# Five K loads and two dk stores of an attention backward kernel, each cut by rows into three transfers

## The chip, the cores and the metric

The kernel runs on one core of a Trainium2 chip. The core has five instruction streams, TensorE (PE, whose weight loads are listed as PEld), VectorE (DVE), ScalarE (ACT), GpSimd (POOL) and SyncE (SP), and 16 DMA engines that move data between HBM and the on-chip SBUF. SP and GpSimd only start transfers here; the DMA engines carry them out. The metric is the device time of one execution in microseconds (us). Before the change the median of three runs is 1271.71 us (1270.49 to 1273.73).

## The reference

The reference is one decode step of softmax attention together with its backward pass. There are 2 x 32 = 64 heads; each has one query row, 8192 keys and values of width 128, all in bfloat16:

```python
B, H, Sq, Sk, D = 2, 32, 1, 8192, 128
def _fwd_reference(q, k, v):
    scale = q.shape[-1] ** -0.5
    scores = jnp.einsum("bhqd,bhkd->bhqk", q, k) * scale
    p = _softmax(scores, axis=-1)
    return jnp.einsum("bhqk,bhkd->bhqd", p, v)

def reference(q, k, v, grad_out):
    _out, _vjp = jax.vjp(_fwd_reference, q, k, v)
    return (_out, *_vjp(grad_out))
```

The outputs are the attention output, dq, dk and dv. K, V, dk and dv are 134 MB each, so 268 MB are read and 268 MB are written; q, grad_out, out and dq are 16 KB each.

## The kernel before, in words

**Tiles.** A head's K (or V) is one tile of 128 rows (the 128 partitions of the SBUF) by 64 x 128 elements: row p holds 64 consecutive keys, 16 KB. A tile is 2 MB. There are twelve such tiles in SBUF (`NTILE = 12`), enough for six heads. Head i+6 is loaded into the tiles of head i, with K and V exchanged (`slot_of`): K of head i+6 goes where V of head i was.

**Work on a head.** TensorE transposes the tile in chunks of 16 keys per row (L220), ScalarE copies each chunk out (L222), and TensorE multiplies it with q or grad_out into scores (L241). VectorE and ScalarE do the softmax. TensorE accumulates out and dq from the original tiles (L401). Then VectorE overwrites the V tile with dv and the K tile with dk (`outer`, L456), and the tile is stored.

**Order.** One loop over chunk steps g interleaves up to four heads, eight steps to a head; every instruction is pinned to its written order on its engine.

**Transfers and their queues.** SP starts all large loads (`load`, L100), in order. Each takes a whole tile, except for K of head 0, which is cut along the row into three. GpSimd starts the stores (L474), in order: dv of head i, dk of head i, dv of head i+1 and so on. Only the last head's stores are cut into quarters and started by SP. A load must wait until the store that frees its tile has landed. Each queue also has eight completion semaphores that it uses in turn, so that a transfer waits for the one eight places before it on its own queue.

**Stores by rows.** `SPREAD` names heads 6, 18, 30, 42 and 54. Their dk is stored by `by_rows` (L89) as two transfers, of 126 and of 2 rows. In this helper `max_dma_last_dim` leaves a row as two pieces of 4096 elements, 8 KB each. Near the start, GpSimd resets the cursor of its transfers and loads 6 of the 64 rows of q (`FIRST = 6`, L112); SP loads the other 58 rows.

Of the kernel before, what the change touches and what calls it, by code (L numbers as in the profile page):

```python
# [20 lines left out]
NTILE = 12  # L21
FIRST = 6
SPREAD = range(6, 60, 12)


@with_exitstack
def kernel(
# [24 lines left out]
    load_eng = nc.sync  # L52
    store_eng = nc.gpsimd
# [26 lines left out]
    def slot_of(i, w):  # L80

        n = 2 * i + w
        return n if n < NTILE else slot_of(i - NTILE // 2, 1 - w)

    def by_rows(eng, dst, src, rows):

        p = 0
        for m in rows:
            pin(eng.dma_start(out=dst[p : p + m], in_=src[p : p + m], max_dma_last_dim=NT * D))  # L89
            p += m  # L90

    def load(i, w, pieces=(NCH,)):
        h = heads[i]
        t = kvp.tile([P, NT, D], BF16, tag=f"kv{slot_of(i, w)}", name="kvt")
        h.tile[w] = t
        src = (v_v if w else k_v)[i]
        c = 0
        for m in pieces:
            n0, n1 = c * CH, (c + m) * CH
            pin(load_eng.dma_start(out=t[:, n0:n1, :], in_=src[:, n0:n1, :]))  # L100
            c += m

    load(0, 0, (1, 1, 2))

    qd_nat = evp.tile([P, CH, P], BF16, tag="ev", name="qd_nat")
    for w, a in enumerate((q, grad_out)):
# [9 lines left out]
        pin(load_eng.dma_start(out=qd_nat[r0:BH, w, :], in_=rows[r0:BH]))  # L116

    load(0, 1)
    for j in range(1, min(NTILE // 2, BH)):
        load(j, 0)  # L120
        load(j, 1)
# [328 lines left out]
    def outer(i, w, c, ends):  # L450

        h = heads[i]
        n0 = c * CH
        shape = [P, CH, D // 2, 2]
        pin(
            nc.vector.tensor_tensor(  # L456
                out=h.tile[w][:, n0 : n0 + CH, :].rearrange("p n (e t) -> p n e t", t=2),
                in0=h.qb[w][:]
                .rearrange("p (e t) -> p e t", t=2)
                .unsqueeze(1)  # L460
                .to_broadcast(shape),
                in1=h.pair[w][:, n0 : n0 + CH, :].unsqueeze(2).to_broadcast(shape),
                op=ALU.mult,
            )
        )
        if c + 1 in ends:
            at = ends.index(c + 1)
            b0, b1 = (ends[at - 1] if at else 0) * CH, (c + 1) * CH
            dst = (dv_v if w else dk_v)[i]
            if w == 0 and i in SPREAD:  # L470
                by_rows(store_eng, dst, h.tile[w], (P - 2, 2))
            else:
                eng = load_eng if len(ends) > 1 else store_eng
                pin(eng.dma_start(out=dst[:, b0:b1, :], in_=h.tile[w][:, b0:b1, :]))  # L474
# [12 lines left out]
    for g in range(SL * BH + O0 + NCH + 4 - SL):  # L487
# [15 lines left out]
        if x := within(O1):  # L503
            outer(x[0], 1, x[1], last if x[0] == BH - 1 else whole)
        if x := within(O0):
            outer(x[0], 0, x[1], last if x[0] == BH - 1 else whole)
        ev = None
        if g < SL * BH:
            i, r = divmod(g, SL)
# [84 lines left out]
```

## Time and profile before

| What | Value |
|---|---|
| median of the runs | 1271.71 us |
| time of the profiled execution | 1271.48 us |
| its span, first to last instruction | 1269.7 us |
| PE / DVE / ACT / POOL busy | 85% / 80% / 43% / 6% |
| HBM read and written over the span | 423 GB/s |
| SP's queue (q1): packets, MB, share of 16 engines | 20172, 272.70, 50.4% |
| GpSimd's queue (q0): packets, MB, share of 16 engines | 19216, 264.25, 49.0% |
| whole-tile store, issue to landing (median) | 66.1 us |
| whole-tile load, issue to landing (median) | 20.1 us (V), 20.3 us (K) |

The span is measured from the first to the last instruction; 1.8 us of the profiled execution lie outside it. A DMA queue's share says how much of the time of all 16 engines its packets took. A packet is one contiguous piece, here mostly a 16 KB row. A busy share of an engine is an average; an idle engine costs nothing unless it is the one that the end waits for.

### The profile page before, as it was taken

The page shows a single profiled execution, that of the slowest core. Times are in us where ns is not written, and L with a number is a line of the kernel's source. Part 1 is how long each engine was busy: PE and PEld are TensorE (multiplying, and loading weights), DVE is VectorE, ACT ScalarE, POOL GpSimd, SP SyncE. Part 2 cuts the span into 40 slices and gives each one's busy share as a digit, 9 for nine tenths or more (in the row PEclk, how much of TensorE's full clock was granted, in tenths as well). Part 3 has the DMA queues.
Part 4 walks back from the last instruction along what each step waited for, and adds up shares of the span by engine and source line. Part 5 has one row for each costly group of instructions (what it writes and reads, how often), then busy time and mean ns, then how long its engine had stood idle before and what let it go on. Part 6 is the DMA issues. An engine that isn't in the chain of part 4 may idle for free.

```text
span 1269.7 us, 24553 instructions
## 1 busy us (share of the span) xinstructions
PE 1073.2 (85%) x10056; PEld 757.9 (60%) x10056; DVE 1020.8 (80%) x2269; ACT 552.0 (43%) x769; POOL 72.9 (6%) x138
## 2 busy tenths in 40 slices
PE   6999999999888997988897888888888889898870
PEld 4666666666656665666565656555655656565540
DVE  3889998998878898788787878788878887796882
ACT  3545444444434444444343444444434444444430
POOL 0000000000000000000000000000000000000000
PEclk9999999999999999899899999999989999998995
DMA  9999999999999999999999999999999999999997
GB/s 392 427 429 428 428 428 429 429 429 429 430 428 429 428 429 432 428 429 429 430 424 425 429 429 428 429 429 428 424 428 431 428 429 429 428 430 426 430 426 294
DMA packets 39501, 538.53 MB, mean 424 GB/s; under 512 B 4956, under 2 KB 4956, under 8 KB 6236
## 3 DMA queue, kind: packets, MB, share of 16 engines
q1 hardware_dynamic: 20172, 272.70, 50.4%
q0 software_dynamic: 19216, 264.25, 49.0%
q8 instruction: 79, 1.29, 0.4%
q14 instruction: 34, 0.28, 0.1%
HBM read 268.47 MB, written 268.47 MB: 423 GB/s over the span
## 4 chain that ended last, share of the span: by engine, by line
DMA 33%; another core or an unknown queue 22%; DVE 17%; PE 13%; issue 9%; ACT 2%; SPq 1%; POOL 1%; ACTq 0%; POOLq 0%; DVEq 0%
DMA kvt<-in_v_dram 18%; DMA kvt<-in_k_dram 10%; DVE kvt L456 9%; PE tp L220 8%; DMA out_dram<-kvt 4%; DVE sel L424 3%; DVE rows L254 2%; PE acc L401 2%; PE raw L241 2%; ACT ev L222 1%; SPq L100 1%; DVE sel L418 1%; PE sw L261 1%; DVE pair L335 1%
## 5 line engine op out<-in xcount | busy, mean ns | idle before, releaser
L222 ACT COPY ev<-tp 128x1024 f32<-128x1024 f32 x512 | 518.6, 1013 | 665.5 <-PE tp L220 659.3
L220 PE MATMUL tp<-ident_f,kvt 128*128 128x128 f32 x4096 | 566.2, 283 | 96.0 <-DMA kvt<-in_v_dram 70.5
L456 DVE TENSOR_TENSOR kvt<-qb,pair 128x2048 bf16<-128x2048 bf16 x512 | 616.9, 1216 | 0.1
L220 PEld LDWEIGHTS tp<-ident_f,kvt 128*128 128x128 f32 x4096 | 470.2, 147 | 216.5 <-issue 170.6
L241 PE MATMUL raw<-ev,qwin 128*32 128x512 bf16 x2048 | 210.3, 400 | 0.0
L254 DVE COPY rows<-raw 128x512 f32<-128x512 f32 x128 | 88.0, 688 | 91.9 <-PE raw L241 91.7
L424 DVE SCALAR_TENSOR_TENSOR sel<-acc,diag,sel 128x128 f32<-128x128 f32 x384 | 134.7, 351 | 13.6
L261 PEld LDWEIGHTS sw<-sel,rows 128*128 128x128 f32 x1024 | 125.5, 193 | 30.4 <-DVE sel L418 15.2
L261 PE MATMUL sw<-sel,rows 128*128 128x16 f32 x1024 | 138.0, 267 | 0.5 <-DVE st L355 0.5
L474 POOL DMA_DIRECT2D out_dram<-kvt x121 | 64.7, 534 | 1106.3 <-DVE kvt L456 507.3
L401 PE MATMUL acc<-kvt,dS_pad 128*32 128x512 bf16 x1024 | 107.3, 410 | 0.8 <-DVE dS_pad L387 0.8
L401 PE MATMUL acc<-kvt,E_pad 128*32 128x512 bf16 x1024 | 103.0, 392 | 0.7 <-DVE E_pad L312 0.7
L202 PE MATMUL sw<-ident_f,qT 128*128 128x128 bf16 x128 | 29.1, 227 | 55.3 <-DVE st L275 55.1
L347 PEld LDWEIGHTS sw<-st,ones 128*128 128x128 f32 x256 | 38.4, 189 | 56.2 <-issue 54.5
L241 PEld LDWEIGHTS <-qwin 128*32 128x32 bf16 x2048 | 54.0, 95 | 5.4 <-issue 1.0
L347 PE MATMUL sw<-st,ones 128*128 128x1 f32 x256 | 49.3, 262 | 0.5 <-DVE st L318 0.5
L280 DVE TENSOR_REDUCE st<-sw 1x1 f32<-1x128 f32 x64 | 17.9, 279 | 37.8 <-PE sw L279 37.8
L401 PEld LDWEIGHTS <-dS_pad 128*32 128x32 bf16 x1024 | 26.4, 94 | 36.2 <-issue 29.1
L401 PEld LDWEIGHTS <-E_pad 128*32 128x32 bf16 x1024 | 26.3, 93 | 33.7 <-issue 28.8
L438 PEld LDWEIGHTS acc<-ones,sel 128*128 128x128 f32 x256 | 39.8, 197 | 8.1 <-DVE sel L424 8.1
L312 DVE CAST E_pad<-E_f 128x64 bf16<-128x64 f32 x64 | 12.5, 195 | 38.9 <-ACT E_f L303 38.9
L418 DVE TENSOR_SCALAR sel<-acc,diag 128x128 f32<-128x128 f32 x128 | 43.7, 342 | 0.0
(53 smaller groups left out, 399.3 us busy)
## 6 DMA issues: line engine op xcount, KB each, us to landing
out_dram<-kvt POOLq DMA_DIRECT2D x121, 2048.0 KB, 66.1
kvt<-in_v_dram SPq DMA_DIRECT2D x64, 2048.0 KB, 20.1
kvt<-in_k_dram SPq DMA_DIRECT2D x63, 2048.0 KB, 20.3
out_dram<-kvt POOLq DMA_DIRECT2D x5, 2016.0 KB, 71.2
out_dram<-kvt SPq DMA_DIRECT2D x8, 512.0 KB, 23.9
kvt<-in_k_dram SPq DMA_DIRECT2D x2, 512.0 KB, 4.3
kvt<-in_k_dram SPq DMA_DIRECT2D x1, 1024.0 KB, 6.9
out_dram<-kvt POOLq DMA_DIRECT2D x5, 32.0 KB, 70.5
```

The source lines that it names most:

```text
L220: pin(nc.tensor.transpose(tp[:, m, :], two, ident_f[:]))
L222: pin(nc.scalar.copy(out=ev[:], in_=tp[:]))
L241: nc.tensor.matmul(h.raw[g * SW : (g + 1) * SW, :], lhsT=qwin[:, w, e, q0 : q0 + SW], rhs=cols[:, b, :, e], start=(c == 0), stop=(c == NCH ...
L254: pin(nc.vector.tensor_copy(out=h.rows[:], in_=h.raw[:]))
L261: nc.tensor.matmul(h.score[w].rearrange("p (n m t) -> p n m t", m=QT, t=2)[:, :, m, :], lhsT=h.rows[:, m * P : (m + 1) * P], rhs=sel4[:].r ...
L347: nc.tensor.matmul(out, lhsT=ones[:].to_broadcast([P, P]), rhs=col, start=True, stop=True)
L401: nc.tensor.matmul(h.acc[w][g : g + CW, :], lhsT=wts[:, n0 : n0 + CW], rhs=rows[:, n0 : n0 + QT, :].rearrange("p n d -> p (n d)"), start=( ...
L418: nc.vector.tensor_scalar(out=h.sel[:], in0=block, scalar1=diag[:, 0:1], scalar2=None, op0=ALU.mult)
L424: nc.vector.scalar_tensor_tensor(out=h.sel[:], in0=block, scalar=diag[:, b : b + 1], in1=h.sel[:], op0=ALU.mult, op1=ALU.add,)
L438: nc.tensor.matmul(h.acc[w][:, 0:1], lhsT=h.sel[:], rhs=ones[:], start=True, stop=True)
L456: nc.vector.tensor_tensor(out=h.tile[w][:, n0 : n0 + CH, :].rearrange("p n (e t) -> p n e t", t=2), in0=h.qb[w][:] .rearrange("p (e t) -> ...
L474: pin(eng.dma_start(out=dst[:, b0:b1, :], in_=h.tile[w][:, b0:b1, :]))
```

## The change

Seven of the whole-tile transfers are cut by rows into three. On SP: K of heads 9, 11, 13, 15 and 17, as 112 rows and two smaller parts. On GpSimd: dk of heads 8 and 12. They all go through `by_rows`, so a row becomes two 8 KB pieces (a part of one row stays in one piece). Order, engines and the work on the data stay as they were. SP starts ten more transfers and GpSimd four more. The lines below the new constants move down by two, those behind the new lines in `load` by five, and those behind the new branch in `outer` by seven.

```diff
 SPREAD = range(6, 60, 12)
+LOAD_ROWS = {9: (112, 8, 8), 11: (112, 12, 4), 13: (112, 14, 2), 15: (112, 10, 6), 17: (112, 15, 1)}
+STORE_ROWS = {8: (112, 8, 8), 12: (112, 12, 4)}
@@ in load
         src = (v_v if w else k_v)[i]
+        if w == 0 and i in LOAD_ROWS:
+            by_rows(load_eng, t, src, LOAD_ROWS[i])
+            return
         c = 0
@@ in outer
             if w == 0 and i in SPREAD:
                 by_rows(store_eng, dst, h.tile[w], (P - 2, 2))
+            elif w == 0 and i in STORE_ROWS:
+                by_rows(store_eng, dst, h.tile[w], STORE_ROWS[i])
             else:
```

## The prediction

> **What bounds the kernel now.** I read the page's slices first, then the DMA table, then the waits of the two issuing queues, then the end in windows.
>
> ```profile
> span 1269.7 us, 24553 instructions
> DMA  9999999999999999999999999999999999999997
> q1 hardware_dynamic: 20172, 272.70, 50.4%
> q0 software_dynamic: 19216, 264.25, 49.0%
> ```
>
> The 16 DMA engines are busy in every slice but the last; the two queues fill 99.4% of their time. No compute engine does (PE 85%, DVE 80%). So bytes per DMA engine set the time. A 16 KB row costs one engine 16384 x 16 x 0.504 x 1269.7 / 272.70 MB = 0.615 us (the packet records: mostly 0.611).
>
> ```profile
> SPq L100 <- DMA out_dram<-kvt: 1126.0, 116, 27.4
> POOL out_dram L474 <- DMA out_dram<-kvt: 104.1, 12, 13.9
> POOL out_dram L89 <- DMA out_dram<-kvt: 1.2, 1, 1.2
> 150.00:250.00 100.00, 93.07 (x896) 65.94 (x889) 90.46 (x202) 49.27 (x68) 7.26 (x13) 0.98 1.01 429
> 250.00:350.00 100.00, 89.43 (x866) 63.53 (x866) 86.48 (x194) 47.45 (x67) 5.85 (x11) 1.00 1.01 429
> ```
>
> SP waits for stores to free tiles nearly all the time; GpSimd lost 104 us to the landing of earlier stores and the DMA share (last column but one) stayed at 1.01 in these windows, in which the stores and most of the loads of the change fall. Waits of the issuers are covered by queued transfers.
>
> ```profile
> 1240.00:1245.00 5.00, 1.00 (x9) 0.13 (x1) 4.89 (x9) 0.00 (x0) 0.00 (x0) 0.50 1.02 433
> 1245.00:1250.00 5.00, 0.90 (x3) 0.63 (x3) 0.72 (x4) 0.00 (x0) 0.00 (x0) 0.50 0.96 401
> 1250.00:1255.00 5.00, 0.00 (x0) 0.00 (x0) 0.00 (x0) 0.00 (x0) 0.00 (x0) 0.50 0.90 374
> 1255.00:1260.00 5.00, 0.00 (x0) 0.00 (x0) 0.00 (x0) 0.00 (x0) 0.00 (x0) 0.50 0.64 267
> 1260.00:1265.00 5.00, 0.00 (x0) 0.00 (x0) 0.00 (x0) 0.00 (x0) 0.00 (x0) 0.50 0.47 193
> 1265.00:1269.70 4.70, 0.00 (x0) 0.00 (x0) 0.00 (x0) 0.00 (x0) 0.00 (x0) 0.50 0.11 42
> ```
>
> Compute is over at 1247 us. From there the DMA share falls in steps: engines run dry one after another, and the last one sets the end. The trace keeps the times of the 16 increments (one per engine) of each transfer. Those of the last small store come at 1251.7, 1253.0, 1254.7, 1254.8, 1255.5, 1257.1, 1259.6, 1259.9, then 1264.3, 1265.8, 1266.3, 1266.4, 1266.5, 1266.7, 1266.8 and 1268.2 us. Eight engines are early, eight late; the mean is 1261.1. A perfectly even spread would save 7.1 us. **So the question is which engines gain rows and which lose them.**
>
> **Which engine gets which row.** I put the packet records into 16 sequences (each packet starts 3 to 4 ns before the end of the one before it on its engine; where two fit, the pattern of eight rows and a 4-byte completion decides). They show: a 128-row transfer is 8 rows per engine; the 58-row load of q on SP went to two engines, 29 rows each; GpSimd's 6-row load put one row on each of six engines, those two among them; each 126-row store put 9 rows on 14 engines, and its 2-row companion one row on each of the other two, the same two all five times. So rows are dealt in equal shares to the largest number of engines, up to 16, that divides them, and GpSimd's small parts go on from where the last ended (14 + 2 = 16 comes back). Of the two spared engines one is slow: its rows took 0.620 us as loads and 0.631 as stores, against 0.612 and 0.615.
>
> **The five loads.** 112 rows are 7 per engine, and a part of m rows one row on each of m engines, instead of 8 on all. If all SP parts start at the same engine, the sums over the five loads, in the order of engines, are +5, +4, +3, +3, +2, +2, +1, +1, -1, -1, -2, -2, -3, -3, -4, -5 rows (21 moved). If they rotate as GpSimd's do, each load deals 16 rows in turn and the sum is 0. The sequences show only one SP transfer that did not use all engines, so both stay possible; I take the same start: it gives the wider bounds, and the kernel resets a cursor for GpSimd alone. Bounds: the last engine gets +5 rows, +3.1 us; at best the eight late ones are the eight that lose, paired as well as can be, and the end moves to 1265.3, -2.9 us. Between them: the two engines of the q load (+5, +4) ended by 1260, so they stay harmless. Of the two that end last, one is among the six of the 6-row load (the sequences leave open which), so with a common start it would get +2 or +3 rows: 1266.8 + 1.2 = 1268.0 up to 1268.2 + 1.8 = 1270.0, against 1268.2 now. That is 0 to +1.8; I take the middle, **+0.9 us**.
>
> [...]
>
> **The two stores.** 7 rows on all engines, then 8 + 8 or 12 + 4 = 16 rows dealt in turn: 0, and the cursor returns. If GpSimd's parts started at one engine instead, this would add at most 2 rows, 1.2 us, either way.
>
> **Packets and completions.** An engine handles some 40 rows of the split loads and 16 of the split stores as two packets: 2 x 0.309 - 0.611 us less one more overlap of 3.5 ns is 3.5 ns each, 0.2 us. 14 more transfers bring 4-byte completions of 9 ns, and the SPREAD windows show some four extra per engine for small parts: under 0.2 us. **+0.4 us** together.
>
> **Issue and waits, costed at nothing.** SP starts ten more transfers at 0.33 us, GpSimd four more at 0.5 to 0.8. The second and third part each wait for the semaphore used eight transfers before; behind them stand the next V load on SP and the next dv store on GpSimd, and K loads of later heads wait for that store. A load there lands 30 us after issue; even with every second K load cut, eight places are some 50 us, so those have landed 20 us earlier. On GpSimd at 190 to 300 us a store lands 43 to 50 us after issue and one is issued every 9.5 us: five in flight, seven with two small ones, under eight. The cover is the queue: from a store's issue to its first increment 20 us pass at 110 us, where the first split load is issued, and 35 from 190 us on. A K load in 8 KB pieces that takes turns with 16 KB store packets takes 16 x (0.306 + 0.608) = 14.6 us instead of 9.7 in the engine; five times 4.9 us later would be 24 us if nothing covered it, but the engine moves stores meanwhile, so what is late next is a dk store by 5 us, inside the 20.
>
> **Sum.** 1271.48 (the profiled execution; the median is 0.23 above) + 0.9 + 0.4 = **1272.8 us**.
>
> **Rival A, slower: the spared pair moves.** If the parts of a split store don't bring GpSimd's cursor back to where it was, the four SPREAD stores after head 12 spare another pair. The slow engine then takes 9 rows instead of 1 four times: 32 x 0.62 = 20 us, and ends at 1259.6 + 20 = 1279.4 instead of 1259.6; with the last engine at 1268.2 that is +11.2, **1283 us**. It decides from two lost SPREADs on (8.6 us of slack are 14 rows). For it: no record shows a part of 8, 12 or 4 on GpSimd. Against: 6, 126 and 2 rows follow the simple count five times.
>
> **Rival B, faster: the late eight are the eight that lose,** and GpSimd's parts start at one engine too: the eight then lose 2, 2, 3, 3, 5, 5, 6 and 7 rows, and paired as well as can be the end moves to 1264.6: -3.6, with the overhead **1268.3 us**. Against: one of the two last engines is near the start. More than 7.1 us less the overhead, 1264.8, no dealing of rows can give.
>
> **Rival C, slower: the cover fails.** A split load or store makes the DMA share drop between 110 and 400 us. It decides once a wait outlasts the 20 to 35 us; GpSimd's longest was 13.9, and one more of that size on top would cost up to its own length: 1277 to **1286 us**. Against: 12 such waits cost no share before.
>
> **How the numbers follow.** Forecast 0.69, A 0.11, B 0.08, C 0.07, something unnamed 0.05. 0.3%, 3.8 us, is about what a measurement of this kernel can tell from no change: 1267.9 to 1275.5. The row bounds of -2.9 and +3.1 with the overhead are 1269.0 to 1275.0, inside it. B lies just inside it as well, and the scatter of the runs (1.6 us) would show it as faster about every second time. So slower 0.20 (A, C and half the unnamed), faster 0.07 (half of B and of the unnamed), same 0.73. The range takes in those bounds, B and the mild end of C, and leaves out A: 1268.0 to 1277.0.
>
> **What would show it.** Right: DMA share 1.01 up to 1240, five K loads of 1792 KB and 14 small parts in the DMA table, increments of the last store that shift by at most 3.1 us each, the two q engines later by 2.5 to 3 us. Wrong: one increment alone 10 us behind all others (A), a window of 100 us below 428 GB/s between 110 and 400 us (C), or all late increments earlier by 2 us or more (B).

## The result, and the profile after

The change made the kernel slower by four to five microseconds. The median of six runs is 1276.36 us (1274.66 to 1278.14) against 1271.47 us (1270.26 to 1273.73) of six runs of the kernel before. The ratio is 1.0039, with a 95% interval of 1.0025 to 1.0053: +4.9 us, between +3.2 and +6.7. The prediction's 1272.8 us was 3.6 us too low. Its range (1268.0 to 1277.0) held the time, but the ratio lies above the 0.3% that it called "no change", though the interval reaches down to 0.25%; to the slower side it had given a chance of 0.20. The profiled execution took 1275.63 us, 4.15 more than that of before; its span grew by 4.2 us.

The page of the kernel after, its first line, its slices of DMA share and of GB/s, and its queues:

```profile
span 1273.9 us, 24586 instructions
DMA  9999999999999999999999999999999999999997
GB/s 392 424 429 429 426 419 411 422 420 420 427 429 428 430 429 428 431 428 428 430 429 427 431 429 428 430 429 427 423 430 428 429 429 430 428 429 427 430 424 295
q1 hardware_dynamic: 20891, 272.70, 50.4%
q0 software_dynamic: 19600, 264.25, 49.0%
```

The bytes of both queues are those of before, the DMA engines are busy throughout as before, and the queues' shares are the same. What moved is the third line: slices 6 to 10 (some 160 to 320 us) carry 411 to 422 GB/s, where before and in most later slices it is 427 to 431. In that stretch the packets of the five loads and the two stores move. The same windows as in the prediction (columns: window, its length, busy time and count on PE, PEld, DVE, ACT and POOL, PE clock, DMA share, GB/s):

```profile
150.00:250.00 100.00, 91.67 (x824) 65.04 (x822) 82.96 (x186) 45.14 (x63) 8.12 (x14) 0.91 1.01 417
250.00:350.00 100.00, 81.96 (x765) 58.06 (x762) 76.73 (x168) 41.46 (x58) 6.23 (x12) 0.93 1.01 422
```

Before, both windows showed a DMA share of 1.01 and 429 GB/s. Now the share is still 1.01 and the GB/s have fallen to 417 and 422. If the engines waited, both would fall. Here only the bytes fell, so the engines were busy and **their packets took longer**. The granted PE clock is lower as well (0.91 and 0.93 against 0.98 and 1.00), and PE did fewer matmuls; but PE was not the bound in either kernel, since the DMA engines had no gap. (A kernel further below, 25 loads in 8 KB pieces, has a clock of 0.86 in a window and keeps 429 GB/s there.)

The packet records say how much longer. Before, a 16 KB packet of a whole tile mostly took 0.611 us and an 8 KB piece 0.309 us. I add up what each packet took above that, and divide by 16 engines; this is called the **excess** from here on.

```
                       excess per engine, us     16 KB and 8 KB packets
                       110-340 us   whole run    over by 60 ns, 110-340 us
before                    0.89         6.23                23
after                     4.66         9.73               341
```

The excess grew by 3.5 us in the whole run, and all of that lies in the stretch of the change. The long packets sit where rows of a split load and rows of a whole load are under way together: 325 of the 341, though only 46% of the packets of the stretch run at such a moment. While a split load is under way and no whole one (11% of the packets), hardly any is long (3 of the 341). Of the 341, 216 belong to stores.

The end of the kernel after:

```profile
1245.00:1250.00 5.00, 1.06 (x9) 0.13 (x1) 4.89 (x9) 0.00 (x0) 0.00 (x0) 0.50 1.01 428
1250.00:1255.00 5.00, 0.90 (x3) 0.63 (x3) 0.78 (x4) 0.00 (x0) 0.00 (x0) 0.50 0.96 402
1255.00:1260.00 5.00, 0.00 (x0) 0.00 (x0) 0.00 (x0) 0.00 (x0) 0.00 (x0) 0.50 0.83 346
1260.00:1265.00 5.00, 0.00 (x0) 0.00 (x0) 0.00 (x0) 0.00 (x0) 0.00 (x0) 0.50 0.60 250
1265.00:1270.00 5.00, 0.00 (x0) 0.00 (x0) 0.00 (x0) 0.00 (x0) 0.00 (x0) 0.50 0.43 176
1270.00:1273.90 3.90, 0.00 (x0) 0.00 (x0) 0.00 (x0) 0.00 (x0) 0.00 (x0) 0.50 0.07 29
```

The shares tell when the average engine ends. After: 1250 + 5 x (0.96 + 0.83 + 0.60 + 0.43) + 3.9 x 0.07 = 1264.4 us. Before, in the same way from the rows in the prediction: 1245 + 5 x (0.96 + 0.90 + 0.64 + 0.47) + 4.7 x 0.11 = 1260.4 us. So **the average engine ends 4.0 us later**, though it moves the same bytes: 3.5 us of excess and about the 0.4 us that the prediction had for packets and completions. (The packets' times alone, added up, grew from 1261.9 to 1266.1 us per engine, 4.2; with some 1,100 more packets, that each overlap the one before by 3.5 ns, 0.2 of this is counted twice.) The last engine's final completion moved from 1267.7 to 1272.4 us, by 4.7. Redealing rows cannot move the average; this alone tells that the main cost is not which engine has which row.

Rows of the DMA waits of the issuing engines in the kernel after (engine, line, what it waited for: us in total, times, longest):

```profile
POOL out_dram L481 <- DMA out_dram<-kvt: 28.6, 3, 11.9
...
SPq L91 <- DMA out_dram<-kvt: 39.4, 5, 9.3
SPq L91 <- DMA kvt<-in_k_dram: 32.8, 4, 10.9
```

The split transfers do wait on SP, up to 10.9 us at a time for an earlier load, by the program for the semaphore that it still holds. With the share at 1.01, none of it reached the DMA engines.

### The profile page after: what moved, and what is told of

Read it like the earlier page. It is cut to its first block, busy times and chain, and to the rows that moved or that the text cites. A ratio compares the mean times of both kernels' runs of the same rounds, so it can differ in the third digit from the quotient of the medians.

```text
span 1273.9 us, 24586 instructions
## 1 busy us (share of the span) xinstructions
PE 1072.7 (84%) x10056; PEld 757.6 (59%) x10056; DVE 1021.0 (80%) x2269; ACT 552.3 (43%) x769; POOL 75.9 (6%) x142
## 4 chain that ended last, share of the span: by engine, by line
DMA 38%; DVE 23%; PE 15%; issue 11%; another core or an unknown queue 10%; ACT 2%; POOL 1%; SPq 0%; ACTq 0%; POOLq 0%; DVEq 0%
DMA kvt<-in_k_dram 24%; DVE kvt L461 12%; DMA kvt<-in_v_dram 10%; PE tp L225 8%; DMA out_dram<-kvt 3%; DVE sel L429 3%; DVE rows L259 2%; PE acc L406 2%; PE raw L246 2%; ACT ev L227 2%; DVE sel L423 1%; PE sw L266 1%; DVE pair L340 1%; DVE dSu L383 1%
```

## The experiments

The first question was which part of the change costs the time; the second, what about a split makes packets longer; the third, which engine ends last. Kernels measured together share runs of the kernel before, so the comparison value differs a little from group to group.

**The five loads alone.**

```diff
-STORE_ROWS = {8: (112, 8, 8), 12: (112, 12, 4)}
+STORE_ROWS = {}
```

> Only the five split loads, stores as before. The changed kernel took 4.9 us longer; in its trace, packets between 110 and 340 us were longer by 3.8 us per DMA engine in all. Theory P (placement: in a 112-row load a row goes through another DMA engine than in a 128-row load, and packets of two engines slow each other): +4 to +5. Theory R (only the dealing of rows counts, the two split stores are the rest): +1.5 to +2.

Measured: 1276.69 us against 1272.43, ratio 1.0033 (1.0020 to 1.0045), +4.3 us. The excess at 110 to 340 us is 5.55 us. This is what theory P expected, and R did not: the loads carry nearly all of the change's cost. The excess is above the 4.66 of the whole change, so from one profiled run to another it can differ by about 1 us.

**The two stores alone.**

```diff
-LOAD_ROWS = {9: (112, 8, 8), 11: (112, 12, 4), 13: (112, 14, 2), 15: (112, 10, 6), 17: (112, 15, 1)}
+LOAD_ROWS = {}
```

> Only the two split stores, loads as before. P and R with loads as the cause: 0 to +0.7. If the stores carry the loss (cursor, completions, packets): +3 to +5.

Measured: 1273.73 us, ratio 1.0009 (1.0000 to 1.0018): +1.3 us by the medians, anything from 0 to 2.3. The expected 0 to +0.7 lies in that interval, the +3 to +5 does not. The excess at 110 to 340 us is 1.45, 0.56 above that of before. Together with the loads (4.3 + 1.3 = 5.6) this agrees with the change's +4.9 within the intervals.

**Five loads cut evenly.** 112 and 16 rows. Going by the counts that the prediction read from the records (128 rows as 8 to an engine, 126 as 9 on 14 engines), I took both parts to be dealt in equal shares to 16 engines, 7 and 1 rows each, so that no engine gains a row.

```diff
-LOAD_ROWS = {9: (112, 8, 8), 11: (112, 12, 4), 13: (112, 14, 2), 15: (112, 10, 6), 17: (112, 15, 1)}
-STORE_ROWS = {8: (112, 8, 8), 12: (112, 12, 4)}
+LOAD_ROWS = {i: (112, 16) for i in range(9, 18, 2)}
+STORE_ROWS = {}
```

> The same five loads cut as 112 and 16 rows, so that every DMA engine gets 8 rows again (7 + 1); stores as before. P, or theory K (8 KB pieces beside 16 KB packets are what slows): +3 to +4.5, packets between 110 and 340 us longer by some 3.8 us per engine. R, or theory N (parts on fewer than 16 engines push the engines out of step): 0 to +0.5.

Measured: 1274.14 us, ratio 1.0014 (1.0005 to 1.0023), +1.7 us. The last engine ends at 1270.4, 2.7 us later than before, with no row gained by that count. That lies between what P or K (+3 to +4.5) and what R or N (0 to +0.5) expected, and decides for neither; but this split costs something, though by that count every engine keeps its eight rows. Between this and the five loads alone are 2.55 us; but the excess differs as well (3.09 against 5.55 us), so that difference cannot be put down to the dealing of rows alone. The stretch of 110 to 340 us in the kernel before and in this one:

```profile
110.00:340.00 230.00, 211.28 (x2041) 149.97 (x2041) 204.64 (x456) 111.87 (x156) 14.71 (x27) 0.99 1.01 429
```

```profile
110.00:340.00 230.00, 199.45 (x1816) 141.28 (x1814) 182.71 (x405) 99.11 (x139) 13.11 (x24) 0.93 1.01 425
```

And in the five loads alone:

```profile
110.00:340.00 230.00, 197.77 (x1795) 139.48 (x1793) 181.17 (x402) 98.72 (x138) 13.11 (x24) 0.93 1.01 420
```

One share, three rates: 429, 425 and 420 GB/s.

**25 loads in 8 KB pieces, whole.** Five loads move the time by little more than the runs scatter, so the next kernels do the same to every second K load, 25 in all. This one keeps the 128 rows together and takes only the pieces of `by_rows`.

```diff
-LOAD_ROWS = {9: (112, 8, 8), 11: (112, 12, 4), 13: (112, 14, 2), 15: (112, 10, 6), 17: (112, 15, 1)}
-STORE_ROWS = {8: (112, 8, 8), 12: (112, 12, 4)}
+LOAD_ROWS = {i: (128,) for i in range(9, 58, 2)}
+STORE_ROWS = {}
```

> 25 K loads (heads 9 to 57, every second) whole, but in 8 KB pieces, one transfer of 128 rows each. K: 25 x 0.76 = +19 us. P, N and R: 25 x 8 rows x 3.5 ns = +0.7 us.

Measured: 1272.79 us against 1272.43, ratio 1.0005 (0.9995 to 1.0015); the excess of the run is 6.0, as before. The size of the pieces alone costs nothing that shows here. A stretch with a low PE clock, in this kernel, still moves 429 GB/s, so the lower clock after the change is not what made the packets longer:

```profile
410.00:510.00 100.00, 83.67 (x714) 58.95 (x716) 73.15 (x160) 38.65 (x54) 4.78 (x9) 0.86 1.01 429
```

**25 loads cut evenly,** as 112 and 16 rows in 8 KB pieces.

```diff
-LOAD_ROWS = {i: (128,) for i in range(9, 58, 2)}
+LOAD_ROWS = {i: (112, 16) for i in range(9, 58, 2)}
```

> 25 K loads as 112 and 16 rows in 8 KB pieces. P, or K (the 8 KB pieces): 25 x 0.76 = +19 us. N and R: +1 us (pieces and completions alone).

Measured: 1355.85 us against 1272.46, ratio 1.0674 (1.0623 to 1.0724): +83 us, 3.3 us per load, far above the +19 that any theory expected. By the count above no engine has a row more than in the whole loads, and the DMA share stays at 1.01. The stretch of 700 to 1100 us, before and here:

```profile
700.00:1100.00 400.00, 339.52 (x3193) 239.01 (x3189) 323.96 (x714) 175.09 (x244) 23.05 (x42) 0.97 1.01 429
```

```profile
700.00:1100.00 400.00, 323.46 (x2879) 228.33 (x2876) 292.06 (x642) 157.70 (x220) 20.02 (x37) 0.91 1.01 394
```

8% fewer bytes in the same busy time. The excess of the run is 81.0 us per engine, 61.2 of it on loads and 19.9 on stores, which were not touched.

**The same, with a row in one piece of 16 KB.**

```diff
         if w == 0 and i in LOAD_ROWS:
-            by_rows(load_eng, t, src, LOAD_ROWS[i])
+            p = 0
+            for m in LOAD_ROWS[i]:
+                pin(load_eng.dma_start(out=t[p : p + m], in_=src[p : p + m]))
+                p += m
             return
```

> The same 25 loads as 112 and 16 rows, but with rows in one 16 KB piece. P: +19 us, as with 8 KB pieces. K, N and R: 0 to +0.5 us.

Measured: 1328.16 us, ratio 1.0436 (1.0401 to 1.0472), +56 us. The excess is 54.6. So the small pieces do not cause the cost; over 25 cuts they add 28 us to it. Over the first five cuts it is the other way round. At 110 to 340 us the excess is 10.9 us here and 3.9 with 8 KB pieces, and the rates are, here and then with 8 KB pieces:

```profile
110.00:340.00 230.00, 202.01 (x1907) 142.85 (x1907) 191.37 (x424) 104.16 (x145) 13.64 (x25) 0.97 1.01 410
110.00:340.00 230.00, 196.50 (x1803) 138.76 (x1802) 182.53 (x404) 99.21 (x139) 13.11 (x24) 0.93 1.01 423
```

**25 loads as two halves of 64 rows,** in 16 KB pieces: no part is small.

```diff
-LOAD_ROWS = {i: (112, 16) for i in range(9, 58, 2)}
+LOAD_ROWS = {i: (64, 64) for i in range(9, 58, 2)}
```

> The same 25 loads as twice 64 rows, 16 KB pieces, 4 + 4 rows per engine. P, if 64 rows are dealt out in fours from the first row on, so that most rows change engine: +10 to +19 us. K, N and R, or P if a row keeps its engine: 0 to +0.5 us.

Measured: 1323.0 us (1312.5 to 1342.5), ratio 1.0396 (1.0352 to 1.0439), +51 us; the excess is 44.4 in the profiled run, the shortest of the four. The expected +10 to +19 was again too low. A small part is not what costs.

What was left were two theories. Either two transfers in place of one cost it, whatever their shape; or it is the placement: that in every 128-row transfer an engine has the same rows of the tile, and in another cut other rows, which meet those of the neighbouring transfers. The second is a guess about the dealing: no record says which rows an engine has.

**25 loads as two transfers of all 128 rows,** each with half of every row.

```diff
-            load(i + AHEAD, 0)
+            load(i + AHEAD, 0, (2, 2) if i + AHEAD in range(9, 58, 2) else (NCH,))
```

> 25 K loads (heads 9 to 57, every second) cut along the row: two transfers of all 128 rows with half a row (8 KB) each, so that there are two transfers to a tile but every row keeps its DMA engine. Theory P (placement: rows that go through another engine than in the 128-row loads beside them): 0 to +1 us. Theory T (any load in two transfers costs, whatever its rows): as with 64 + 64 rows, +40 to +50 us.

Measured: 1274.22 us against 1272.86, ratio 1.0007 (0.9998 to 1.0016); excess 5.6. As many transfers as in the halves by rows, as many bytes in each, and no cost. The number of transfers is ruled out. What differs is how the rows are cut: 64 at a time (by the count four to an engine) against 128 (in the records of the kernel before, eight to an engine). The stretch of 700 to 1100 us, first as halves by rows, then as halves of each row:

```profile
700.00:1100.00 400.00, 340.03 (x3055) 238.81 (x3054) 308.83 (x680) 167.91 (x235) 21.62 (x40) 0.93 1.01 411
```

```profile
700.00:1100.00 400.00, 346.87 (x3217) 245.13 (x3217) 323.29 (x716) 176.61 (x247) 23.51 (x43) 0.95 1.01 428
```

**21 dk stores cut evenly,** the loads whole. (The expectation says 20; the `STORE_ROWS` below name 21 heads, and the DMA table of the run has 21 such stores.)

```diff
-LOAD_ROWS = {9: (112, 8, 8), 11: (112, 12, 4), 13: (112, 14, 2), 15: (112, 10, 6), 17: (112, 15, 1)}
-STORE_ROWS = {8: (112, 8, 8), 12: (112, 12, 4)}
+LOAD_ROWS = {}
+STORE_ROWS = {i: (112, 16) for i in range(8, 58, 2) if i not in SPREAD}
```

> 20 dk stores on GpSimd (every second head from 8, without those that are stored as 126 + 2) as 112 and 16 rows; all loads whole. If placement costs only where SBUF is written (loads): 0 to +2 us. If stores collide as loads do: +30 us or more.

Measured: 1309.28 us at the median, with a wide scatter (1294 to 1321); the ratio, taken from the three shortest of its five runs, is 1.0169 (1.0151 to 1.0186), so +22 us at least. The expectation of 0 to +2 missed. The excess is 38.7, of which 35.9 are on the stores and 2.8 on the loads. GpSimd waited 21 times, 183.5 us in all, for earlier stores, and still the DMA share did not drop:

```profile
POOL out_dram L91 <- DMA out_dram<-kvt: 183.5, 21, 13.3
700.00:1100.00 400.00, 329.39 (x3050) 232.73 (x3049) 307.19 (x677) 166.95 (x233) 27.46 (x48) 0.94 1.01 410
```

So the cost is not particular to loads or to SP's queue. That the change's own two stores cost little fits their number only.

How well the excess accounts for the time, profiled run by profiled run (the time over the shared median of before, the excess over the 6.23 us of before):

```
                                time, us   excess, us
the change                        +4.2        +3.5
the five loads alone              +3.6        +4.1
the two stores alone              -1.7        +0.6
5 loads 112 + 16, 8 KB            +1.7        +2.2
the same at heads 29 to 37        +1.2        +1.3
25 loads 112 + 16, 8 KB          +81.0       +74.8
25 loads 112 + 16, 16 KB         +54.3       +48.4
25 loads 64 + 64, 16 KB          +40.1       +38.2
21 stores 112 + 16, 8 KB         +36.4       +32.5
25 loads whole, 8 KB              +4.1        -0.2
25 loads in half rows             +0.5        -0.7
```

In the four rows that add 36 us or more, 89 to 95% of the added time are longer packets. The rows with five loads, the change among them, agree within 0.7 us, and the two stores' 2.3 us are about the scatter of the runs. One row does not fit: the profiled run of the 25 whole loads was the slowest of its ten, and its 4.1 us are not longer packets. It had the lowest granted clock of the ten (0.934), TensorE was still at work shortly before the end, and for some us the DMA engines had little to do:

```profile
1250.00:1255.00 5.00, 3.74 (x37) 2.28 (x37) 4.05 (x10) 1.71 (x4) 0.53 (x1) 1.00 0.19 79
```

**Two engines with 12 rows more.** Behind twelve of the K loads, SP starts an additional transfer of two rows. I took it that each of these starts at the same engine, as both parts of 8 rows of the load of head 9 did in the changed kernel, and that this is where the 58-row load of q starts; then two engines get some 7.2 us each (12 x 0.6). No record names the engines. The rows are written to the place of the last head's dk, which the last store overwrites, so the outputs are unchanged.

```diff
             load(i + AHEAD, 0)
+            if i + AHEAD in range(9, 33, 2):
+                pin(load_eng.dma_start(out=dk_v[BH - 1][0:2, 0:63], in_=k_v[i][0:2, 0:63]))
```

> The kernel before, and behind 12 of its K loads one more transfer on SP, two rows of 15.75 KB from K to a place of dk that the last store overwrites: 12 rows, some 7.2 us, more work on the two engines that the 58-row load of q used. By the tracing of the packets these two end by 1260 us and the last engine at 1268: 0 to +0.5 us. If the last engine is one of them: +7 us.

Measured: 1272.18 us against 1272.86, ratio 0.9993 (0.9985 to 1.0002): nothing.

**Four engines with 12 rows more.**

```diff
-                pin(load_eng.dma_start(out=dk_v[BH - 1][0:2, 0:63], in_=k_v[i][0:2, 0:63]))
+                pin(load_eng.dma_start(out=dk_v[BH - 1][0:4, 0:63], in_=k_v[i][0:4, 0:63]))
```

> The same with four rows instead of two: 12 rows, 7.2 us, more on four engines. If the engine that ends last is the third or fourth in SP's order, as the tracing of the changed kernel suggests: +6 to +7.5 us. If the last two are further on: 0 to +0.7 us.

Measured: 1280.12 us, ratio 1.0066 (1.0045 to 1.0086), +7.3 us by the medians. In its profile one engine ends at 1276.9 us, and all others by 1268.2:

```profile
1265.00:1270.00 5.00, 0.00 (x0) 0.00 (x0) 0.00 (x0) 0.00 (x0) 0.00 (x0) 0.50 0.27 110
1270.00:1278.70 8.70, 0.00 (x0) 0.00 (x0) 0.00 (x0) 0.00 (x0) 0.00 (x0) 0.50 0.05 19
```

A share of 0.05 of 16 engines is one engine for most of those 8.7 us. If these 48 rows went round all 16 engines, each would get three, 1.8 us, and no engine would be that late alone. So, with one start for all these transfers, the first two engines in that order have slack, and one of those that end late in the kernel before is the third or the fourth; that it is the very last one fits best (1267.7 + 7.2 = 1274.9 us, against 1276.9 here). By the prediction's sums, the change's five loads give that place three rows more.

**Five loads cut evenly, later.** The five loads here cost 0.34 us each (1.7 / 5), the 25 cost 3.3. One theory was that the price grows with the distance between the engines: while they keep in step the placements do not meet, and early in the run they are closer: the 16 increments of a store of the kernel before spread over 2 to 7 us between 110 and 340 us, where the loads of heads 9 to 17 move, and over 20 to 33 us between 540 and 760 us. So the same five cuts were made at heads 29 to 37.

```diff
-LOAD_ROWS = {9: (112, 8, 8), 11: (112, 12, 4), 13: (112, 14, 2), 15: (112, 10, 6), 17: (112, 15, 1)}
-STORE_ROWS = {8: (112, 8, 8), 12: (112, 12, 4)}
+LOAD_ROWS = {i: (112, 16) for i in range(29, 38, 2)}
+STORE_ROWS = {}
```

> Five K loads as 112 and 16 rows as in the even cut of heads 9 to 17, but at heads 29, 31, 33, 35 and 37, where the DMA engines are further apart in their queues (a store's 16 increments spread over 20 us there, against 6 to 7 at heads 9 to 17). If a split load has its own price: +1.7 us as there. If the price grows with the distance between the engines: +8 to +16 us, the 25-load kernels' 2 to 3.3 us per load.

Measured: 1273.18 us against 1272.49, ratio 1.0004 (0.9995 to 1.0013), +0.5 us (-0.6 to +1.7). The excess at 540 to 760 us is 2.78 against 1.41 before. That theory falls: late cuts are no dearer than early ones. In 8 KB pieces the price grows with the number of cuts. With 25 of them the excess is 3.9 us at 110 to 340, 29.8 at 340 to 700 and 34.3 at 700 to 1100 us: the first few cost about what five cost, the later ones several times that.

In 16 KB pieces the price does not grow. The five cuts at 110 to 340 us add 10.0 us of excess to the 0.89 of before (112 + 16) and 8.2 (64 + 64), 2.0 and 1.6 us each; all 25 add 48.4 and 38.2, 1.9 and 1.5 each. So the low price of the first five cuts belongs to the 8 KB pieces, in which all five-load kernels here were cut. Why is open. Late loads alone are not the reason: in the kernel of 25 whole loads in 8 KB pieces a K load lands 64.5 us after its issue, against 20.3 before, and costs nothing.

No kernel here beat the kernel before.

## Why the prediction was right or wrong

**The bound: right.** The DMA engines set the time in every kernel above whose median is clearly longer: the stretches shown have a share of 1.01, and with four rows more one engine alone sets the end.

**The step that failed: the price of a row.** The prediction took a row at 0.615 us whatever transfer it came in, and under "Packets and completions" allowed 0.4 us for all that a cut adds. In the change a packet took longer when other transfers were cut: 3.5 us per engine of longer packets had no term in the sum. The trace of before would have shown only a little of it: while its five stores of 126 + 2 rows are under way the excess is 1.2 us, against 0.7 at the rate of the other times, so 0.1 us for each. One sign of being right failed with it: the last engine moved by 4.7 us, where the prediction allowed 3.1. The prediction asked what the new dealing of rows could gain or lose and what ten and four more transfers add, not whether two transfers of other rows could be dearer than one of 128. The 25 halves of 64 rows show that they can be: +51 us. That the time still fell inside the range is luck: the bounds of the prediction's own terms end at 1275.0 us, only the mild end of Rival C carried the range on to 1277.0, and C is not what happened.

**The five loads: mechanism right, size most likely at the upper bound.** The dealing was as taken: with the packet records of the change put into 16 sequences again, eight engines have 18 pieces of 8 KB of the load of head 9 and eight have 14, so both parts of 8 rows went to the same eight engines; dealt in turn, every engine would have 16. For the other four loads the common start stays the choice that the forecast made. If the last engine is, as the kernel with four longer engines suggests, the third or fourth, it gains three rows: 3 x 0.615 = 1.85 us, the upper end of the 0 to +1.8, where +0.9 was taken. The last engine's 4.7 us are then 1.85 for rows, 0.4 for packets and completions, and some 2.4 of stretch, which is only what is left over and not measured on that engine. An engine that loses rows need not end earlier, since the stretch comes on top.

**The two stores: nearly right.** 0 was forecast; 0 to +2.3 was measured, and 0.56 us of excess. Their parts brought the cursor back: in the records of the change the slow engine is one of the spared pair all five times, as before.

**Issue and waits: right.** SP's split parts waited up to 10.9 us for a transfer and GpSimd up to 11.9, inside the 20 to 35 us of cover, and the DMA share stayed at 1.01.

**Rival A, the spared pair moves: false.** The slow engine ended at 1263.9 us, not last.

**Rival B, faster: false.** The late engines gained as well as lost, and the average engine went up by 4.0 us; B could only deal a fixed sum.

**Rival C, the cover fails: false, though its sign came.** The prediction had named a window of 100 us below 428 GB/s as what would show it. Two appeared, at 417 and 422, and they mean something else: C was a drop in the DMA share, and the share did not drop. The sign was badly chosen, as longer packets lower the GB/s too; share and GB/s have to be read together.

**Placement: how far it is shown.** The runs show that 25 loads which keep all 128 rows in each transfer cost nothing (whole in 8 KB pieces 1.0005, half rows 1.0007), and 21 to 25 cuts by rows 1.017 to 1.067. The long packets of the change lie where split and whole loads meet. Why it should be dear for an engine to have other rows is not shown: no record here names the engine or the row of a packet, so placement is what the runs leave over, not what they show at work. If an engine does get other rows, it gets them on the side of HBM as well as of SBUF, and no run here tells the two apart.

## What to carry to other kernels

In this kernel, which the DMA engines bound, 25 loads cut along the row cost nothing (1.0007) and 25 cut by rows 51 to 83 us. In another that they bound, try first the large transfers at all 128 rows of the tile, cut along the row where a cut is needed. Read the DMA share and the GB/s of a window side by side: a share that held while the bytes fell (1.01 at 394 to 425 GB/s) meant longer packets here, and neither waits nor the number of rows per engine explained them. Where a sum goes by a price per row, allow for that price to change when the shape of the transfers does.

## What was unexpected in the hardware

- With loads cut by rows, the packets of transfers that were not cut got longer: of the 81.0 us of excess with 25 cut loads, 19.9 were on stores, whose cuts were those of before and which had 4.7 there.
- In 8 KB pieces the cost of one even cut is far from constant: 0.1 to 0.35 us with five loads, 3.3 us with 25. In 16 KB pieces it is 1.5 to 2 us of excess from the first five cuts on. Why stays open.
- Pieces of 8 KB cost nothing in 25 whole loads (1.0005) and were dearer in 25 cut ones (+83 us against +56 us in 16 KB pieces), but not in the first few (3.9 against 10.9 us of excess at 110 to 340 us).
- Twelve additional transfers of two rows had no effect (0.9993), twelve of four rows cost +7.3 us: one engine ended 8.7 us after all others and alone set the end.
- The eight engines that end late seem to be those that also carry the instruction queue. In the kernel before that queue moved 79 packets of some 0.96 us; in the sequences of the changed kernel 76 of its 79 fall on the eight engines that end last. Shared by eight that is 9.5 us each, and the prediction's two groups of eight end 10.6 us apart on average. (Where two sequences fit a packet the tracing can err.)

```profile
q8 instruction: 79, 1.29, 0.4%
```
